# Ten decode units beside attention, two staging and result buffers, and another order of silu and output blocks

## The chip, the cores and the metric

The kernel runs on one core of one Trainium2 chip. The metric is the device time of a launch in microseconds, as the median of several runs.

## The reference

Attention over q, k, v (4 batches, 8 heads, 576 positions, 64 wide) has two parts that are added: a coarse attention on positions averaged in fours, repeated four times along the sequence, and a local one with a band of width 3 to either side. Its output, 2304 tokens of 512, goes through two dense layers:

```python
a = x @ w1                      # 512 -> 1024
b = x @ w2                      # 512 -> 1024
x = ((a * b) @ w3) @ w_out      # 1024 -> 1024 -> 512
h = x @ w_in                    # 512 -> 2048
out = (h * (1.0 / (1.0 + np.exp(-h)))) @ w_out2   # 2048 -> 512
```

The weights arrive as 64-bit floating point numbers.

## The kernel before

**Numbers.** The weights are decoded on the chip from 64-bit to 32-bit values with integer operations (absolute value on ScalarE, clamp, shift and two merges on VectorE). Where a product is to be exact enough, each operand is split in a high and a low part (hi, lo), and TensorE makes three products (hi·hi, lo·hi, hi·lo; `PASSES`).

**Opening (to about 111 us).** w3 @ w_out is made into one matrix (`wprime`, L449), while the first of the 16 attention units run.

**Middle (111 to 504 us).** A unit u of attention is two heads of one batch. Its work is cut in 48 steps: `scores(u)` (D1, L1), `turn(u)` (D2, L2: transposes; `pool_v`: two adds on GpSimd that make `vd`, L236 and L239) and `sums(u - 1)` (D3, L3). D3 (L304) multiplies the transposed coarse weights `EdT` (two ScalarE copies, L298) with `vd` into one of two PSUM buffers and copies the result out on VectorE (L316); L3 (L369) makes the local part, and `make_x` adds both. In between lie 192 slots: an ab slot is 12 matmuls of one half of x against w1 or w2 (L540), a y slot 12 matmuls of (a·b) with the joined matrix (L580), for 320 or 256 tokens. y goes to DRAM (`ydram`).

**Background decode.** The second layer pair's weights are 16 units (`units`: 8 of w_in, 8 of w_out), each loaded to a staging tile (`bg_load`, `sw`, 1 MB in two DMAs), decoded and split (`bg_steps`), and stored to DRAM (`wsd`, `wod`) from a result tile (`res`). A unit of w_in has two results, one of 768 and, after sums of its blocks (`mix`), one of 1024 columns. The staging tile and the result tile have one buffer each in the pool `stg`; the decoded values alternate between two. `starts` says at which slot each unit begins: 14 + 18n for six units, 122 + 6n for ten. The steps stand 1 to 11 slots behind that, the load of the next unit behind the last merge.

**What sets the order.** Outside the last stage the framework places instructions by priority and by the time at which it expects their inputs; each engine then runs its own list strictly in order. `behind` puts the steps of a slot no earlier than the last marked instruction of the slot ahead; it does not bound them from the other side. All DMAs are issued by SyncE, in order.

**Turn to the last stage.** At slot `bg_end` (185) `open_y` closes the pool `stg` and opens `yp` in its place; y of the first tile of 768 tokens is loaded there (`y_load`), combined on GpSimd (`y_mix`, L752) and split (`y_high`, ScalarE, L757; `y_rest`, VectorE or GpSimd, L763).

**Last stage (from L956, order written out by hand on TensorE, VectorE, ScalarE, GpSimd).** Three tiles of 768 tokens times eight units of 256 hidden columns. A unit (`h_unit`) makes its 2x2 block product with seven chains of 6 matmuls (L916, a Strassen-like scheme) on two PSUM buffers, and VectorE sums them (L905) to the halves `cf` (ready after chain 4) and `cg` (after chain 6). `silu` takes the sigmoid on ScalarE (L886); `rest`, one chain later, multiplies (L891), rounds (L892), and subtracts the low part on GpSimd (L893). Behind each chain follow `run_out` blocks: a block is three matmuls (L852) of the unit before's half and a quarter of w_out, first the first half's six, then the second's. At a tile's end, in the first unit of the next one, the six accumulators are evicted (L859, L861) and stored.

Of the kernel before, what the change touches and what calls it, by code (L numbers as in the profile page):

```python
# [8 lines left out]
F32 = mybir.dt.float32  # L9
F32R = mybir.dt.float32r  # L10
# [19 lines left out]
I32 = mybir.dt.int32  # L30
# [5 lines left out]
def tile_model(ctx: ExitStack, tc: tile.TileContext, qk, vw, vr, w12, w3t, wo, wb, out):  # L36
# [3 lines left out]
    def pool(stack, name, side, space=None, bufs=1):  # L40
        kw = {} if space is None else {"space": space}
        return stack.enter_context(
            tc.tile_pool(name=name, bufs=bufs, side=side, reuse_waits="tile", **kw)
        )
# [3 lines left out]
    wpool = pool(ctx, "wpool", "left", bufs=4)  # L48
    s_stg, s_att, s_x, s_w3, s_c = (ExitStack() for _ in range(5))
    stg = pool(s_stg, "stg", "left", bufs=2)  # L50
    s_stg2, s_cb = ExitStack(), ExitStack()
    att = pool(s_att, "att", "left", bufs=2)
    stg2 = pool(s_stg2, "stg2", "left", bufs=2)
    xpool = pool(s_x, "xpool", "right", bufs=12)
    w3pool = pool(s_w3, "w3pool", "right", bufs=2)

# [59 lines left out]
    n_loads = [0]  # L116

    def stage(home, name):
        return home.tile([P, 2, 512, 2], I32, tag="st", name=name, bufs=1)

    def load_w(key):
        n = n_loads[0]
        home = homes[n % len(homes)]
        n_loads[0] += 1
        if not wide:
            st = home.tile([P, 2, 512], F32, tag="st", name="st", bufs=1)
        elif n < 4 or 6 <= n < 10:
            st = wpool.tile([P, 2, 512, 2], I32, tag="wB" if n < 4 else "wC", name="lent")
        else:
            st = stage(home, "st")  # L130
        for t in range(2):
            src = w_source(key, t)
            if wide:
                nc.sync.dma_start(st[:, t].rearrange("p n w -> p (n w)"), src.bitcast(I32))
            else:
                nc.sync.dma_start(st[:, t], src)
        raw[key] = st
# [270 lines left out]
    def turn(u):  # L408
        D2(u)
        L2(u)  # L410
        pool_v(u)
        load_vr(u + 1)
        pool_qk(u + 1)

    def sums(u):
        D3(u)
        L3(u)
        load_vw(u + 1)

# [76 lines left out]
        else:  # L496
            load_to(n + 2)

    homes.append(stg2)
    load_qk(0)  # L500
    load_to(1)
    load_vr(0)
# [115 lines left out]
    def bg_load(n):  # L618
        if n >= len(units):
            return  # L620
        kind, p = units[n]
        if wide:
            st = stg.tile([P, 2, 512, 2], I32, tag="st", name="sw", bufs=1)
        else:
            st = stg.tile([P, 2, 512], F32, tag="st", name="sw", bufs=1)
        for t in range(2):
            src = wb[2 * p + kind, :, t * 512:(t + 1) * 512]
            if wide:
                nc.sync.dma_start(st[:, t].rearrange("p n w -> p (n w)"), src.bitcast(I32))
            else:  # L630
                nc.sync.dma_start(st[:, t], src)
        bg["st", n] = st

    def bg_steps(n):

        kind, p = units[n]
        hold = {}

        def first():
            st = bg.pop(("st", n))  # L640
            v = stg.tile([P, 1024], I32, tag=("dec", "dec2")[n % 2], name="dec", bufs=1)
            hold["v"], hold["f"] = v, v.bitcast(F32)
            if wide:
                st = st.rearrange("p t n w -> p (t n) w")
                hold["st"] = st
                nc.scalar.activation(hold["f"], st[:, :, 1].bitcast(F32), AF.Abs)
            else:
                nc.scalar.copy(hold["f"], st.rearrange("p t n -> p (t n)"))

        def clamp():  # L650
            if wide:
                nc.vector.tensor_scalar(
                    out=hold["f"], in0=hold["f"], scalar1=E_LOW, scalar2=E_HIGH,
                    op0=ALU.max, op1=ALU.min,
                )
                nc.vector.tensor_scalar(
                    out=hold["v"], in0=hold["v"], scalar1=3, scalar2=0x3FFFFFF8,
                    op0=ALU.logical_shift_left, op1=ALU.bitwise_and,
                )

        def top():
            if wide:
                nc.vector.scalar_tensor_tensor(
                    out=hold["v"], in0=hold["st"][:, :, 1], scalar=-0x40000000, in1=hold["v"],
                    op0=ALU.bitwise_and, op1=ALU.bitwise_or,
                )

        def low():
            if wide:
                nc.vector.scalar_tensor_tensor(  # L670
                    out=hold["v"], in0=hold["st"][:, :, 0], scalar=29, in1=hold["v"],
                    op0=ALU.logical_shift_right, op1=ALU.bitwise_or,
                )
            bg_load(n + 1)

        def high(w):
            hold["r"] = stg.tile([P, 2, 1024], F32R, tag="res", name="res", bufs=1)[:, :, :w]
            nc.scalar.copy(hold["r"][:, 0], hold["f"][:, :w])  # L678

        def rest(w):  # L680
            r = hold["r"]
            nc.vector.tensor_tensor(  # L682
                out=r[:, 1], in0=hold["f"][:, :w], in1=r[:, 0].bitcast(F32), op=ALU.subtract
            )

        def store(where):
            nc.sync.dma_start(
                where.rearrange("p (l n) -> p l n", l=2), hold["r"].bitcast(F32)
            )

        def mix():
            f = hold["f"]
            a11, a12, a22, a21 = (f[:, 256 * i:256 * i + 256] for i in range(4))
            for out_, in0, in1, op in (
                (a22, a21, a22, ALU.add), (a21, a11, a21, ALU.subtract),
                (a11, a22, a11, ALU.subtract), (a12, a12, a11, ALU.subtract),
            ):
                nc.vector.tensor_tensor(out=out_, in0=in0, in1=in1, op=op)

        steps = [(0, first), (1, clamp), (2, top), (3, low)]  # L700
        if kind:
            steps += [(5, lambda: high(1024)), (6, lambda: rest(1024)),
                      (7, lambda: store(wod[p]))]
        else:
            steps += [(5, lambda: high(768)), (6, lambda: rest(768)),
                      (7, lambda: store(wsd[p, :, 0:1536])), (7, mix),
                      (9, lambda: high(1024)), (10, lambda: rest(1024)),
                      (11, lambda: store(wsd[p, :, 1536:3584]))]
        return steps

    plan = {}
# [1 line left out]
    def at(slot, fn):  # L713
        plan.setdefault(slot, []).append(fn)

    starts = [14 + 18 * n for n in range(6)] + [122 + 6 * n for n in range(10)]
    at(13, lambda: bg_load(0))
    for n in range(len(units)):
        for k, fn in bg_steps(n):
            at(starts[n] + k, fn)  # L720
# [68 lines left out]
    end_a = max(i for i, g in enumerate(kinds) if g is not None)  # L789

    def open_y():
        s_stg.close()
        yp.append(pool(ctx, "yp", "left"))
        y_load(0)
# [20 lines left out]
    for i, slot in enumerate(slots):  # L815
        run_plan(36 + i)
        if i == 13:
            assert n_jobs[0] == len(jobs)
            s_stg2.close()
            homes[:] = [stg]  # L820
            cpool_b[0] = pool(s_cb, "cpool_b", "right", bufs=2)
        behind(plan.pop(i, []))
        slot()
        n = 36 + max(0, i - 3) if i < 40 else 72 + ((i - 39) * 36) // 46
        run_steps(n // 3 + 1)
        if not opened and done_steps[0] == NSTEP:
            s_att.close()
            opened = True
            assert i < bg_end, (i, bg_end)
    for i in sorted(plan):  # L830
        behind(plan.pop(i))
    assert opened
# [51 lines left out]
    def silu(u, half, c):  # L884
        sg = temp("sg", f"{u}_{half}", 2, 2 * NH)
        nc.scalar.activation(sg, c, AF.Sigmoid)  # L886
        g = b2.tile([P, 2, 2 * NH], F32R, tag="g", name=f"g{u}_{half}", bufs=5)
        G[u, half] = g

        def rest():  # L890
            nc.vector.tensor_tensor(out=sg, in0=c, in1=sg, op=ALU.mult)  # L891
            nc.vector.tensor_copy(g[:, 0], sg)  # L892
            nc.gpsimd.tensor_tensor(  # L893
                out=g[:, 1], in0=sg, in1=g[:, 0].bitcast(F32), op=ALU.subtract
            )

        after(1, rest)

    def h_unit(u):
        t, p = divmod(u, 8)  # L900
# [8 lines left out]
        for i, (name, w, c) in enumerate(CH):  # L909
# [38 lines left out]
                after(3, lambda i=i: y_rest(t + 1, i))  # L948
            if 2 <= p < 6 and i == 5 and t + 1 < NT:
                y_mix(t + 1, p - 2)  # L950
            run_out((2, 2, 2, 2, 2, 1, 1)[i])
        wc_load(u + 2)
        if p == 1 and t + 1 < NT:
            y_load(t + 1)
# [2 lines left out]
    with tc.manual_schedule(engines={E.PE, E.DVE, E.Activation, E.Pool}):  # L957
        for u in range(NUN):
            h_unit(u)
            assert not todo  # L960
            todo.extend((u, half, j) for half in range(2) for j in range(6))
        for _ in range(3):
            next_chain()
        assert not later
        todo.sort(key=lambda x: (x[2], x[1]))
        run_out(12)


# [54 lines left out]
```

## Time and profile before

| | |
|---|---|
| Median of 3 runs | 967.16 us (966.91 to 969.13) |
| Profiled execution | 970.69 us |
| its span | 968.9 us |
| its mean granted TensorE clock | 0.962 |
| TensorE busy | 874.4 us, 90% of the span |
| VectorE, ScalarE, GpSimd busy | 536.6, 300.2, 282.4 us |

The span is what the trace covers, from the first instruction to the last; 1.8 us lie around it. Times in the trace count from the span's start. "Busy" of TensorE is not its best rate, since matmuls overlap; its rate is read from starts of equal groups. L12 is line 12 of the kernel before.

### The profile page before, as it was taken

How to read it: one execution, taken by the hardware profiler on the slowest of the kernel's cores; microseconds unless marked ns; L12 is line 12 of the kernel's file. 1: busy time of each engine (PE TensorE's matmuls, PEld its weight loads, DVE VectorE, ACT ScalarE, POOL GpSimd, SP SyncE). 2: the span in 40 equal slices, each digit the busy share in tenths (PEclk: the TensorE clock that was granted, in tenths of full speed). 3: DMA queues.
4: the chain of work that ended last, by engine and by line, in shares of the span. 5: the costliest groups of instructions: out<-in, count | busy, mean ns of one | idle time of the engine just before them, and what ended most of it. 6: DMA issues, size and time to landing. Idle time of an engine off the chain costs nothing.

```text
span 968.9 us, 17419 instructions
## 1 busy us (share of the span) xinstructions
PE 874.4 (90%) x7104; PEld 761.9 (79%) x7104; DVE 536.6 (55%) x850; ACT 300.2 (31%) x865; POOL 282.4 (29%) x226
## 2 busy tenths in 40 slices
PE   3999999999999999999970699999899999999996
PEld 2555689889998999999870578888788888888884
DVE  5999987545546462766552444545536456543432
ACT  5665654543344444333221211113111022111101
POOL 2000244333424242311210622434314335121311
PEclk9999989999999999999995599999999999999998
DMA  9926544343341521368789332424624232632403
GB/s 341 336 92 206 180 146 135 120 148 114 131 168 56 196 97 64 130 228 307 262 296 366 126 128 76 153 76 145 210 80 151 77 128 101 164 130 76 153 0 66
DMA packets 39729, 149.17 MB, mean 154 GB/s; under 512 B 4448, under 2 KB 11616, under 8 KB 33504
## 3 DMA queue, kind: packets, MB, share of 16 engines
q1 hardware_dynamic: 39648, 148.05, 45.1%
q8 instruction: 56, 0.92, 0.4%
q14 instruction: 25, 0.20, 0.1%
HBM read 115.52 MB, written 32.51 MB: 153 GB/s over the span
## 4 chain that ended last, share of the span: by engine, by line
PE 60%; DVE 15%; DMA 9%; POOL 6%; issue 4%; ACT 4%; SPq 0%; POOLq 0%; ACTq 0%; DVEq 0%
PE o L852 17%; PE h L916 13%; PE ab L540 13%; PE y L580 7%; POOL g L893 4%; DMA sw<-wb 4%; PE wp L449 4%; PE ol L369 2%; DVE sg L891 2%; DMA wsd<-res 1%; DVE g L892 1%; DVE u L905 1%; PE tl L345 1%; DVE cg L905 1%; ACT band L250 1%
## 5 line engine op out<-in xcount | busy, mean ns | idle before, releaser
L852 PE MATMUL o<-wo,g 128*128 128x512 f32 x864 | 238.1, 403 | 24.3 <-POOL g L893 23.0
L852 PEld LDWEIGHTS o<-wo,g 128*128 128x128 f32 x864 | 160.7, 190 | 59.3 <-POOL g L893 32.3
L893 POOL TENSOR_TENSOR g<-sg,g 128x768 fp32r<-128x768 f32 x48 | 88.1, 1835 | 277.9 <-DVE g L892 277.9
L916 PE MATMUL h<-yc,wcb 128*128 128x384 f32 x576 | 120.1, 345 | 8.3 <-POOL yc L763 6.6
L916 PEld LDWEIGHTS h<-yc,wcb 128*128 128x128 f32 x576 | 106.6, 193 | 17.4 <-POOL yc L763 7.1
L916 PE MATMUL h<-yc,wca 128*128 128x384 f32 x432 | 90.7, 346 | 30.7 <-ACT yc L757 28.7
L565 POOL TENSOR_TENSOR c<-cf,c 128x320 fp32r<-128x320 f32 (+1 forms) x64 | 66.5, 1039 | 172.0 <-DVE c L564 145.1
L540 PE MATMUL ab<-x,w_wB 128*128 128x320 f32 (+1 forms) x768 | 112.5, 301 | 0.8 <-ACT x L393 0.4
L540 PE MATMUL ab<-x,w_wA 128*128 128x320 f32 (+1 forms) x768 | 111.7, 302 | 1.4 <-DVE cf L554 0.6
L580 PE MATMUL y<-c,w_wC 128*128 128x320 f32 (+1 forms) x768 | 109.0, 298 | 2.3 <-POOL c L565 1.3
L916 PEld LDWEIGHTS h<-yc,wca 128*128 128x128 f32 x432 | 79.8, 193 | 38.3 <-ACT yc L757 28.9
L540 PEld LDWEIGHTS ab<-x,w_wA 128*128 128x128 f32 x768 | 105.5, 192 | 3.3 <-DVE cf L554 0.8
L540 PEld LDWEIGHTS ab<-x,w_wB 128*128 128x128 f32 x768 | 105.4, 191 | 1.7 <-ACT x L393 0.7
L580 PEld LDWEIGHTS y<-c,w_wC 128*128 128x128 f32 x768 | 103.1, 188 | 3.2 <-POOL c L565 1.6
L886 ACT ACTIVATE sg<-cf 128x768 f32<-128x768 f32 x24 | 20.3, 847 | 224.5 <-DVE cf L905 224.5
L905 DVE TENSOR_TENSOR u<-h,u 128x384 f32<-128x384 f32 x48 | 26.7, 557 | 80.9 <-PE h L916 80.9
L449 PE MATMUL wp<-w_wo,w_w 128*128 128x512 f32 x128 | 62.1, 628 | 2.4 <-DVE w_w L177 2.0
L554 DVE TENSOR_TENSOR cf<-ab,af 128x320 f32<-128x320 f32 (+1 forms) x64 | 28.9, 451 | 55.4 <-PE ab L540 52.2
L886 ACT ACTIVATE sg<-cg 128x768 f32<-128x768 f32 x24 | 20.3, 846 | 87.6 <-DVE cg L905 87.6
L250 ACT ACTIVATE band<-band,sm 128x38 f32<-128x38 f32 x144 | 44.9, 317 | 5.7 <-DVE sm L246 5.2
L682 DVE TENSOR_TENSOR res<-dec,res 128x1024 fp32r<-128x1024 f32 (+1 forms) x24 | 28.1, 1170 | 33.2 <-ACT res L678 33.0
L891 DVE TENSOR_TENSOR sg<-cg,sg 128x768 f32<-128x768 f32 x24 | 35.0, 1458 | 20.4 <-ACT sg L886 20.4
(115 smaller groups left out, 1067.2 us busy)
## 6 DMA issues: line engine op xcount, KB each, us to landing
wcb<-wsd SPq DMA_DIRECT2D x24, 1024.0 KB, 6.2
wca<-wsd SPq DMA_DIRECT2D x24, 768.0 KB
sw<-wb SPq DMA_DIRECT2D x32, 512.0 KB, 4.9
qk<-qk SPq DMA_DIRECT2D x16, 579.0 KB, 4.8
wsd<-res SPq DMA_DIRECT2D x8, 1024.0 KB, 6.1
wod<-res SPq DMA_DIRECT2D x8, 1024.0 KB, 5.7
wo<-wod SPq DMA_DIRECT2D x8, 1024.0 KB, 5.1
st<-w SPq DMA_DIRECT2D x14, 512.0 KB, 5.0
```

Of the source, the lines that this page charges most:

```text
L250: nc.scalar.activation(E[:, j, :], src[:, j, :], AF.Exp, bias=nb[:, j:j + 1], scale=scale, accum_out=sv[:, j:j + 1],)
L449: nc.tensor.matmul(acc, lhsT=w3v[:, k, j * P:(j + 1) * P], rhs=wov[:, k, :], start=(gp == 0 and k == 0), stop=(gp == 3 and k == 1),)
L540: nc.tensor.matmul(acc[:, :N], lhsT=wv[:, i, w, kk, :], rhs=x[:, j, :], start=(n == 0), stop=(n == 11),)
L554: nc.vector.tensor_tensor(out=cf, in0=acc[:, :N], in1=C.pop("af"), op=ALU.mult)
L565: mark(nc.gpsimd.tensor_tensor(out=c[:, 1], in0=cf, in1=c[:, 0].bitcast(F32), op=ALU.subtract))
L580: nc.tensor.matmul(acc[:, :N], lhsT=WP[kf // 2][:, i, kf % 2, ec * P:(ec + 1) * P], rhs=c[:, j, :], start=(kf == 0 and n == 0), stop=(kf = ...
L852: nc.tensor.matmul(acc, lhsT=g[:, a, j * P:(j + 1) * P], rhs=w[:, b, half, :], start=(p == 0 and half == 0 and n == 0), stop=(p == 7 and h ...
L886: nc.scalar.activation(sg, c, AF.Sigmoid)
L891: nc.vector.tensor_tensor(out=sg, in0=c, in1=sg, op=ALU.mult)
L893: nc.gpsimd.tensor_tensor(out=g[:, 1], in0=sg, in1=g[:, 0].bitcast(F32), op=ALU.subtract)
L905: nc.vector.tensor_tensor(out=out_, in0=in0, in1=in1, op=op)
L916: nc.tensor.matmul(acc, lhsT=wc[w][:, a, c, kt * P:(kt + 1) * P], rhs=y[:, b, kt, :], start=(n == 0), stop=(n == 5),)
```

## The change

Two staging buffers serve the whole middle part (the extra pool `stg2`, closed at slot 13, is gone); units are loaded two ahead, one slot behind the last merge. Ten units start at 14 + 11n and six at 130 + 6n, so `bg_end` becomes 169. Once attention is done, a second result buffer in its memory (`late`) alternates with the first. The steps from `high` on come one slot earlier. D3 moves from `sums` to `turn`, ahead of `pool_qk`. In the last stage the first half's `rest` follows its sigmoid at once, the second half's one chain later as before; the last unit's low part is made on VectorE; there is no block behind chain 0 and there are two behind each other chain; the last twelve blocks run in the order first half, second half, no longer by column block.

```diff
     def stage(home, name):
-        return home.tile([P, 2, 512, 2], I32, tag="st", name=name, bufs=1)
+        return home.tile([P, 2, 512, 2], I32, tag="st", name=name, bufs=2)
...
         load_vr(u + 1)
+        D3(u)
         pool_qk(u + 1)
 
     def sums(u):
-        D3(u)
         L3(u)
...
         if wide:
-            st = stg.tile([P, 2, 512, 2], I32, tag="st", name="sw", bufs=1)
+            st = stage(stg, "sw")
...
-            bg_load(n + 1)
 
         def high(w):
-            hold["r"] = stg.tile([P, 2, 1024], F32R, tag="res", name="res", bufs=1)[:, :, :w]
+            home = stg
+            if late:
+                n_res[0] += 1
+                home = (stg, late[0])[n_res[0] % 2]
+            hold["r"] = home.tile([P, 2, 1024], F32R, tag="res", name="res", bufs=1)[:, :, :w]
...
-        steps = [(0, first), (1, clamp), (2, top), (3, low)]
+        steps = [(0, first), (1, clamp), (2, top), (3, low), (4, lambda: bg_load(n + 2))]
         if kind:
-            steps += [(5, lambda: high(1024)), (6, lambda: rest(1024)),
-                      (7, lambda: store(wod[p]))]
+            steps += [(4, lambda: high(1024)), (5, lambda: rest(1024)),
+                      (6, lambda: store(wod[p]))]
...
-    starts = [14 + 18 * n for n in range(6)] + [122 + 6 * n for n in range(10)]
+    N_EARLY = 10
+    starts = [14 + 11 * n for n in range(N_EARLY)]
+    starts += [130 + 6 * n for n in range(len(units) - N_EARLY)]
+    late, n_res = [], [0]
     at(13, lambda: bg_load(0))
+    at(13, lambda: bg_load(1))
...
             s_att.close()
+            late.append(pool(s_late, "late", "left"))
...
-            nc.gpsimd.tensor_tensor(
+            e = nc.vector if u == NUN - 1 else nc.gpsimd
+            e.tensor_tensor(
                 out=g[:, 1], in0=sg, in1=g[:, 0].bitcast(F32), op=ALU.subtract
             )
 
-        after(1, rest)
+        if half == 0:
+            rest()
+        else:
+            after(1, rest)
...
-            run_out((2, 2, 2, 2, 2, 1, 1)[i])
+            run_out(2 if i else 0)
...
-        todo.sort(key=lambda x: (x[2], x[1]))
         run_out(12)
```

## Rows read from the trace of the kernel before

**Rows 1.** Stages: length, busy us (x instructions) by engine, clock, DMA, GB/s

```profile
111.00:504.00 393.00, 383.47 (x4246) 365.68 (x4242) 227.48 (x405) 155.98 (x517) 130.39 (x131) 0.98 0.47 158
388.00:485.00 97.00, 94.78 (x768) 93.04 (x767) 62.17 (x99) 30.48 (x54) 22.37 (x22) 0.98 0.66 232
...
504.00:557.00 53.00, 14.88 (x49) 12.72 (x49) 19.27 (x23) 11.54 (x15) 16.59 (x9) 0.58 0.69 255
...
948.00:968.90 20.90, 12.46 (x39) 8.55 (x37) 5.06 (x8) 2.60 (x4) 3.61 (x2) 0.77 0.35 76
```

**Rows 2.** Order of time around 504 us: start, length, engine, line [idle before <-releaser]

```profile
495.15 8.78 PE L580 MATMUL y<-c,w_wC 128*128 128x256 f32 x72 [1.06 <-ACT af L547]
...
521.80 0.32 SPq L687 DMA_DIRECT2D wod<-res  x1
...
522.65 2.08 SPq L736 DMA_DIRECT2D yr<-ydram  x2
...
532.68 1.01 PE L916 MATMUL h<-yc,wca 128*128 128x384 f32 x2 [28.74 <-ACT yc L757]
...
545.59 3.57 POOL L763 TENSOR_TENSOR yc<-t,yc 128x768 fp32r<-128x768 f32 x2
...
554.02 2.59 PE L916 MATMUL h<-yc,wca 128*128 128x384 f32 x12
```

**Rows 3.** Groups by line: busy us, mean ns | idle before, by releaser

```profile
L852 PE MATMUL o<-wo,g 128*128 128x512 f32 x864 | 238.1, 403 | 24.3 <-POOL g L893 23.0 <-DVE g L892 0.9 <-PE h L916 0.2
...
L678 ACT CAST res<-dec 128x1024 fp32r<-128x1024 f32 (+1 forms) x24 | 23.5, 979 | 44.0 <-DMA wsd<-res 22.0 <-DMA wod<-res 15.4 <-DVE dec L670 6.7
...
L646 ACT ACTIVATE dec<-sw 128x1024 f32<-128x1024 f32 x16 | 18.2, 1140 | 29.6 <-DMA sw<-wb 27.4 <-DVE w_wA L190 2.2
...
L236 POOL TENSOR_TENSOR vr<-vr 72x512 f32<-72x512 f32 x12 | 17.6, 1463 | 94.4 <-DMA vr<-vr 94.3
...
L311 PE MATMUL od<-EdT,vd 72*64 72x144 f32 x128 | 12.3, 300 | 0.0
```

**Rows 4.** Order of time on SyncE: two of the loads of staged weights

```profile
473.76 1.32 SPq L629 DMA_DIRECT2D sw<-wb  x2
...
501.11 1.35 SPq L629 DMA_DIRECT2D sw<-wb  x2
```

**Rows 5.** Order of time within a unit of the last stage

```profile
564.84 1.22 PE L916 MATMUL h<-yc,wcb 128*128 128x384 f32 x6
...
565.90 1.56 PE L852 MATMUL o<-wo,g 128*128 128x512 f32 x6
...
567.29 1.22 PE L916 MATMUL h<-yc,wcb 128*128 128x384 f32 x6
...
569.20 0.85 ACT L886 ACTIVATE sg<-cf 128x768 f32<-128x768 f32 x1 [10.79 <-DVE cf L905]
...
571.95 0.95 DVE L891 TENSOR_TENSOR sg<-cf,sg 128x768 f32<-128x768 f32 x1
...
573.64 1.83 POOL L893 TENSOR_TENSOR g<-sg,g 128x768 fp32r<-128x768 f32 x1 [11.63 <-DVE g L892]
...
574.93 1.36 DVE L891 TENSOR_TENSOR sg<-cg,sg 128x768 f32<-128x768 f32 x1 [0.97 <-ACT sg L886]
...
575.53 1.43 PE L852 MATMUL o<-wo,g 128*128 128x512 f32 x5 [0.82 <-POOL g L893]
```

**Rows 6.** Order of time on GpSimd: first halves of two successive units

```profile
881.21 1.84 POOL L893 TENSOR_TENSOR g<-sg,g 128x768 fp32r<-128x768 f32 x1 [11.62 <-DVE g L892]
...
898.11 1.84 POOL L893 TENSOR_TENSOR g<-sg,g 128x768 fp32r<-128x768 f32 x1 [11.64 <-DVE g L892]
```

**Rows 7.** Order of time at the end, TensorE's output blocks

```profile
947.71 1.49 PE L852 MATMUL o<-wo,g 128*128 128x512 f32 x4
...
954.05 10.15 PE L852 MATMUL o<-wo,g 128*128 128x512 f32 x32 [1.47 <-POOL g L893]
```

**Rows 8.** Order of time in the second tile's first unit, an h chain

```profile
692.46 1.34 PE L916 MATMUL h<-yc,wca 128*128 128x384 f32 x6 [0.99 <-DVE cg L905]
```

More of the change, by code (lines that the diff above doesn't have):

```diff
@@ L50, in tile_model @@
     stg = pool(s_stg, "stg", "left", bufs=2)
-    s_stg2, s_cb = ExitStack(), ExitStack()
+    s_cb, s_late = ExitStack(), ExitStack()
     att = pool(s_att, "att", "left", bufs=2)
-    stg2 = pool(s_stg2, "stg2", "left", bufs=2)
     xpool = pool(s_x, "xpool", "right", bufs=12)
@@ L125, in load_w @@
         if not wide:
-            st = home.tile([P, 2, 512], F32, tag="st", name="st", bufs=1)
+            st = home.tile([P, 2, 512], F32, tag="st", name="st", bufs=2)
         elif n < 4 or 6 <= n < 10:
@@ L497, in ahead @@
             load_to(n + 2)
-    homes.append(stg2)
     load_qk(0)
@@ L622, in bg_load @@
         if wide:
-            st = stg.tile([P, 2, 512, 2], I32, tag="st", name="sw", bufs=1)
+            st = stage(stg, "sw")
         else:
-            st = stg.tile([P, 2, 512], F32, tag="st", name="sw", bufs=1)
+            st = stg.tile([P, 2, 512], F32, tag="st", name="sw", bufs=2)
         for t in range(2):
@@ L698, in mix @@
                 nc.vector.tensor_tensor(out=out_, in0=in0, in1=in1, op=op)
-        steps = [(0, first), (1, clamp), (2, top), (3, low)]
+        steps = [(0, first), (1, clamp), (2, top), (3, low), (4, lambda: bg_load(n + 2))]
         if kind:
-            steps += [(5, lambda: high(1024)), (6, lambda: rest(1024)),
-                      (7, lambda: store(wod[p]))]
-        else:
[L705 to L708, printed above, removed]
+            steps += [(4, lambda: high(1024)), (5, lambda: rest(1024)),
+                      (6, lambda: store(wod[p]))]
+        else:
+            steps += [(4, lambda: high(768)), (5, lambda: rest(768)),
+                      (6, lambda: store(wsd[p, :, 0:1536])), (6, mix),
+                      (8, lambda: high(1024)), (9, lambda: rest(1024)),
+                      (10, lambda: store(wsd[p, :, 1536:3584]))]
         return steps
@@ L791, in open_y @@
     def open_y():
+        s_late.close()
         s_stg.close()
@@ L818, in tile_model @@
             assert n_jobs[0] == len(jobs)
-            s_stg2.close()
-            homes[:] = [stg]
             cpool_b[0] = pool(s_cb, "cpool_b", "right", bufs=2)
@@ L827, in tile_model @@
             s_att.close()
+            late.append(pool(s_late, "late", "left"))
             opened = True
-            assert i < bg_end, (i, bg_end)
+            assert i < starts[N_EARLY], (i, starts[N_EARLY])
     for i in sorted(plan):
```

## The prediction

> **What bounds the kernel now.** I read the busy times by stage first [rows 1]. From 111 to 504 us TensorE is busy for 383.5 of 393 us, and in the last part of it, 388 to 485 us, for 94.8 of 97: the stage in which attention, ab and y share TensorE is bound by its matmuls. Then 504 to 557 us holds only 49 matmuls at a granted clock of 0.58, where 1.0 is the 2.4 GHz level and 0.5 the 1.2 GHz level: a hole. The last 21 us run at 0.77.
>
> The order of time shows what the hole waits for [rows 2]. The last y matmul ends at 495.15 + 8.78 = 503.9. The last background store (wod) goes out at 521.80, and the load of y, whose buffers lie in the memory of the closed staging pool, at 522.65. TensorE's first h matmul follows at 532.68, after 28.7 us of waiting for ScalarE's half of that y. GpSimd then prepares the other y parts until 545.59 + 3.57 = 549.2. The first product of the second unit ends at 554.02 + 2.59 = 556.6. So background decode is the last thing to end, and all else queues behind it.
>
> Why it is late: ScalarE waited 27.4 us for staged weights (L646) and 22.0 + 15.4 us for the one result buffer to be stored (L678) [rows 3], and loads of the next units go out at 473.76 and 501.11, two units apart, so 13.7 us a unit [rows 4] where the plan allows six slots. A slot is 12 matmuls, 1.5 to 1.8 us (the 72 of 495.15 took 8.78, that is 122 ns each at 256 columns [rows 2]; 320 columns scale to 152).
>
> Last I read one late unit [rows 5]. A chain of 6 h matmuls with two o blocks behind it repeats every 567.29 - 564.84 = 2.45 us, of which the chain alone is 565.90 - 564.84 = 1.06 and the 6 o matmuls 1.39 (232 ns each). In each unit the second o matmul waits for GpSimd's low part of the first half, which starts at 573.64 and takes 1.83: 0.82 us of idle TensorE at 575.53. A unit lasts 898.11 - 881.21 = 16.90 us [rows 6].
>
> **The change, part by part.** (1) *Ten units early, six late, two staging and two result buffers.* Nothing is computed that was not. Four units more lie beside attention, where VectorE is busy 227 of 393 us [rows 1]. With single buffers a unit in the late stage took 13.7 us, and VectorE was busy 62.2 of 97 us there; scaling all of that, the ab work too, to one unit per 9.5 us gives 62.2 x 13.7 / 9.5 = 90 of 97, an upper bound that still fits. So I charge nothing for VectorE; the cover is that TensorE has four accumulators in turn. If it is gone, the price is single waits like those of the stage now, which together are 393 - 383.5 = 9.5 us; I take 0 and keep -3 to +8.
>
> A rule speaks against this part. The row first: the same 128x768 product took 0.95 us alone and 1.36 beside GpSimd's subtraction [rows 5]. The Trainium skill, GPSIMD Engine Reference, section Key points, says that GpSimd shares its SBUF interfaces with VectorE and names contention with VectorE instructions that have two SBUF inputs; the row agrees, and decode has such instructions. If every one of them met GpSimd, the bound of 90 would grow by 1.36 / 0.95 to 129 of 97, the 57 us of the six late units by a third, and the sum would come to about 912; by the row alone, with GpSimd busy 22 of 97 us there [rows 1], it stays.
>
> (2) *The hole.* Slots 160 to 191 end with the last y matmul at 503.9. Counted back at 1.83 us for 320 columns and 1.48 for 256, slot 169, where y is now loaded, begins near 467, and slot 130, the first late unit, near 404. Six units of six slots end near 461, plus a lag I put at 5 to 10 us. The load took 532.68 - 522.65 = 10 us and the preparation 549.2 - 532.7 = 16.5 (GpSimd bound) [rows 2], so y is ready at 467 + 10 + 10 + 16.5 = 503: just in time, with no slack. I put 4 us of lateness (ends 0 and 16). The first unit then costs 7 x 1.06 = 7.4, and one new wait: its first-half silu now stands on VectorE ahead of the sums of chain 5, whose accumulator the second unit's first chain needs. Chain 4 ends at 5.3; sum 0.75, sigmoid 0.95, product 0.95, cast 0.56 and the two sums 1.1 end at 9.7, against 7.4: 2.3 us, once, since later units have o blocks there. With the 1.06 of the next chain that is 503.9 + 4 + 9.7 + 1.1 = 518.7 in place of 556.6: **-38** (-26 to -42).
>
> (3) *Prompt silu and no o blocks behind a unit's first product.* In the new order the first half's product can follow the sigmoid (569.20 + 0.85), about 570.1 instead of 571.95, so GpSimd's part starts about 1.8 us earlier, and the o blocks come one chain (1.06) later: 2.9 us against a wait of 0.82. The wait goes. Late next would be the sums of chain 5, pushed back about 1.6 us behind the product and cast; their accumulator is needed two chains on, 1.06 + 2 x 1.39 = 3.8 us later. A unit becomes 6 x 2.45 + 1.06 = 15.8: 1.1 x 23 = **-25** (-19 if only the visible 0.82 goes; -26). All 24.3 us that L852 waited [rows 3] are of this kind and of the tail.
>
> (4) *The end.* After the last chain's block, at 947.71 + 3 x 0.23 = 948.4, the old order needs the second half at its second block, waits for GpSimd, and runs 32 matmuls from 954.05 in 10.15 us, 317 ns each, at the lower clock [rows 7, 1]. The new order has 18 matmuls of the first half, 4.2 us, while VectorE makes the second half (sum, sigmoid, three passes of 0.56 to 0.95: about 3.9). 36 x 0.232 = 8.4 in place of 964.2 - 948.4 = 15.8; the six evictions then come 0.7 us apart with twelve stores behind them, for which I give back 0.5: **-7**.
>
> (5) *D3 a step earlier.* It issues four pairs of matmuls and a copy as before, and no DMA. Today it never waited (L311, 0.0 idle [rows 3]), as its inputs are a step old. Now TensorE could wait there for GpSimd's two adds behind it (L236 1.46 and a smaller one, at most 2.9 together [rows 3]), with ab matmuls queued behind. Twelve turns lie after the opening (L236 x12): 0 to 35 us, and below nothing by no more than a part of the 9.5 us of waits. I take 0, since outside the last stage instructions are placed where their inputs are expected ready. Where p = 0 a unit also evicts outputs; the first such place cost more than a normal unit (TensorE waited 0.99 at 692.46 [rows 8]); blocks now come closer there, I take -2 (+3 to -4).
>
> **Sum.** 38 + 25 + 7 + 2 = 72 off the span of 968.9 gives 897; with 970.69 - 968.9 = 1.8 around it 899. The median shown is 967.16, 0.36% below that execution: 899 x 0.9964 = 895.5, **895**.
>
> **Rivals.** *The hole closes only in part.* With late units still at 13.7 us, because stores and loads and not the buffers pace them, six end at 404 + 82 = 486, y is ready at 486 + 10 + 16.5 = 513 and TensorE idles 9 to 14 us and restarts at the lower level: 902 to 910, say 905. For it: no slack in part 2. Against it: both waits of ScalarE were on single buffers. *D3 holds TensorE* at most turns: 12 x 2.9 = 35, 930. Against it: L236's inputs are loaded a unit ahead. *The units keep their wait*, because VectorE now stands idle for the sigmoid ahead of the sums and the accumulators come late: 895 + 25 = 920. *Slower than before:* the same place, D3 on TensorE's queue, but each wait long enough that the clock falls to 1.2 GHz behind it, as it did behind the waits of the tail [rows 7]. It decides from 72 / 12 = 6 us a turn: 2.9 of wait and over 6 us of matmuls at half speed. With 7 us a turn the time is 979. The stage now holds a clock of 0.98 with 9.5 us of waits, which speaks against it.
>
> **How the numbers follow.** Forecast (886 to 902) 0.62, hole in part (905) 0.22, D3 (930) 0.07, units (920) 0.06, slower (979) 0.03. The range 885 to 914 takes in the first and nearly all of the second. A measurement of this kernel tells 0.3%, about 3 us, from no change. Every case but the last is faster by far: faster 0.96, same 0.01, slower 0.03.
>
> **What would show it.** Right: the h stage begins within some 5 us of the last y matmul at the 2.4 GHz level; wod's last store goes out before 475; POOL g no longer ends a wait of L852; the unit's period is 15.8; no clock drop in the tail; L311 idle near zero. Wrong: ScalarE's yc still releases the first h matmul after more than 10 us; L311 or L580 with tens of us of idle between 111 and 400; the last y matmul well past 504.

## The result, and the profile after

The changed kernel takes **898.1 us** (median of four, 895.1 to 901.3) where the kernel before took 968.1 in runs beside it: 0.927 of the time (95% interval 0.922 to 0.932). The forecast was 895, its range 885 to 914. The profiled execution is the fastest of the four, 895.1 us, with a span of 893.3 and a mean clock of 0.987; its counterpart of before had 970.7, 968.9 and 0.962. So 75.6 us of span have to be found.

I first read the stages of after, in the same columns as [rows 1]: from and to, length, busy us (x instructions) of TensorE, its weight loads, VectorE, ScalarE and GpSimd, then granted clock, DMA share and GB/s.

```profile
111.00:504.00 393.00, 382.10 (x4288) 363.72 (x4287) 252.60 (x420) 165.39 (x533) 158.97 (x139) 0.98 0.53 186
388.00:485.00 97.00, 94.78 (x776) 93.67 (x775) 65.59 (x93) 32.83 (x57) 38.28 (x29) 0.98 0.57 209
504.00:557.00 53.00, 51.06 (x250) 46.21 (x249) 23.64 (x40) 7.37 (x10) 12.88 (x7) 0.97 0.42 147
877.00:893.30 16.30, 8.85 (x38) 6.76 (x37) 4.55 (x6) 2.34 (x4) 0.00 (x0) 0.91 0.45 97
```

The stage up to 504 is as full as it was, with 25 us more work on VectorE. The hole from 504 to 557 is gone: 250 matmuls at a clock of 0.97 in place of 49 at 0.58. The end no longer runs at 0.77.

The order of time around 504 says what is late now (start, length, engine, line, operation, count, and in brackets the idle time before it and what ended it; SPq is SyncE's queue).

```profile
457.52 0.32 SPq L688 DMA_DIRECT2D wod<-res  x1
...
460.86 0.97 SPq L741 DMA_DIRECT2D yr<-ydram  x2
...
480.63 6.05 PE L538 MATMUL ab<-x,w_wA 128*128 128x256 f32 x36 [1.84 <-ACT yo L587]
...
483.67 1.84 POOL L768 TENSOR_TENSOR yc<-t,yc 128x768 fp32r<-128x768 f32 x1
...
486.51 11.52 PE L578 MATMUL y<-c,w_wC 128*128 128x256 f32 x96
497.87 2.25 PE L925 MATMUL h<-yc,wca 128*128 128x384 f32 x12
...
502.42 0.71 ACT L587 COPY yo<-y 128x256 f32<-128x256 f32 x2 [6.82 <-DMA ydram<-yo]
503.03 0.48 ACT L932 COPY p<-h 128x384 f32<-128x384 f32 x1
503.57 6.03 PE L925 MATMUL h<-yc,wcb 128*128 128x384 f32 x24 [3.44 <-ACT p L932]
509.44 1.21 PE L925 MATMUL h<-yc,wca 128*128 128x384 f32 x6
512.58 2.35 PE L925 MATMUL h<-yc,wca 128*128 128x384 f32 x12 [1.94 <-DVE cg L914]
```

The last background store leaves 64 us earlier than in [rows 2], and GpSimd's last part of y is made by 483.67 + 1.84 = 485.5, 12 us before the first h matmul needs it. That matmul follows the last y matmul (486.51 + 11.52 = 498.0) at once. The largest lateness left is new: ScalarE stands 6.82 us on a yo copy whose buffer is still being stored, the p copy waits behind it in ScalarE's order, and TensorE waits 3.44 us for p. The 24 matmuls after it take 6.03 us, at a lower clock (0.72 from 504 to 510 us).

Last, the groups by line, read as [rows 3], and the unit's period, read as [rows 6].

```profile
L857 PE MATMUL o<-wo,g 128*128 128x512 f32 x864 | 223.8, 395 | 0.0
...
L310 PE MATMUL od<-EdT,vd 72*64 72x144 f32 x128 | 11.4, 299 | 0.0
...
L235 POOL TENSOR_TENSOR vr<-vr 72x512 f32<-72x512 f32 x12 | 20.4, 1701 | 102.7 <-PE od L310 84.3 <-DMA vr<-vr 18.3
...
L644 ACT ACTIVATE dec<-sw 128x1024 f32<-128x1024 f32 x16 | 18.3, 1146 | 2.3 <-DVE w_wA L189 2.3
...
L679 ACT CAST res<-dec 128x1024 fp32r<-128x1024 f32 (+1 forms) x24 | 23.5, 980 | 39.3 <-DVE dec L668 16.3 <-DVE dec L699 12.9 <-DMA wsd<-res 5.9
```

```profile
811.31 1.85 POOL L899 TENSOR_TENSOR g<-sg,g 128x768 fp32r<-128x768 f32 x1 [9.02 <-DVE g L897]
...
827.09 1.85 POOL L899 TENSOR_TENSOR g<-sg,g 128x768 fp32r<-128x768 f32 x1 [9.04 <-DVE g L897]
```

The o matmuls (L852 of before) no longer wait at all, and a unit lasts 827.09 - 811.31 = 15.78 us instead of 16.90. ScalarE's wait for staged weights is gone, and of its waits for the result buffer 5.9 us are left; it waits for VectorE instead. D3's matmuls (L310) still wait for nothing; GpSimd now waits for them, 84 us in all, and between 111 and 400 us TensorE waits for GpSimd for 2.1 us (rows under "D3's place").

**Where the 75.6 us came from.** The first chain of the second unit ends at 556.6 before [rows 2] and at 512.58 + 2.35 - 1.09 = 513.8 after: 42.8. From there to the end of the o block behind the last chain it was 948.4 - 556.6 = 391.8 and is 877.3 - 513.8 = 363.5 (875.88 in the tail below, and six matmuls of 0.23): 28.3. The rest of the span was 20.5 and is 16.0: 4.5.

### The profile page after: what moved, and what is told of

It is laid out like the page before. It is cut to its first block, busy times and chain, and to the rows that moved or that the text cites. A ratio compares the mean times of both kernels' runs of the same rounds, so it can differ in the third digit from the quotient of the medians.

```text
span 893.3 us, 17448 instructions
## 1 busy us (share of the span) xinstructions
PE 852.6 (95%) x7104; PEld 749.6 (84%) x7104; DVE 532.6 (60%) x852; ACT 300.9 (34%) x865; POOL 286.2 (32%) x224
## 4 chain that ended last, share of the span: by engine, by line
PE 81%; DVE 8%; DMA 4%; ACT 2%; issue 2%; POOL 2%; SPq 1%; POOLq 0%; ACTq 0%; DVEq 0%
PE o L857 21%; PE ab L538 20%; PE h L925 19%; PE y L578 9%; PE wp L448 4%; PE ol L368 2%; PE tl L344 1%; PE sd L276 1%; PE s L325 1%; DMA out<-os 1%; PE od L310 1%; PE td L293 1%; DMA ydram<-yo 1%; DMA st<-w 1%; DMA yr<-ydram 1%
## 5 line engine op out<-in xcount | busy, mean ns | idle before, releaser
L857 PE MATMUL o<-wo,g 128*128 128x512 f32 x864 | 223.8, 395 | 0.0
L857 PEld LDWEIGHTS o<-wo,g 128*128 128x128 f32 x864 | 160.3, 188 | 27.2
L899 POOL TENSOR_TENSOR g<-sg,g 128x768 fp32r<-128x768 f32 x46 | 85.0, 1847 | 260.2 <-DVE g L897 244.6
L538 PE MATMUL ab<-x,w_wB 128*128 128x320 f32 (+1 forms) x768 | 114.3, 303 | 3.6 <-POOL x L393 2.1
L563 POOL TENSOR_TENSOR c<-cf,c 128x320 fp32r<-128x320 f32 (+1 forms) x64 | 73.2, 1145 | 117.9 <-DVE c L562 109.3
L925 PE MATMUL h<-yc,wca 128*128 128x384 f32 x432 | 83.6, 337 | 1.9 <-DVE cg L914 1.9
L925 PEld LDWEIGHTS h<-yc,wca 128*128 128x128 f32 x432 | 76.8, 188 | 6.2 <-DVE cg L914 2.3
L235 POOL TENSOR_TENSOR vr<-vr 72x512 f32<-72x512 f32 x12 | 20.4, 1701 | 102.7 <-PE od L310 84.3
L448 PEld LDWEIGHTS wp<-w_wo,w_w 128*128 128x128 f32 x128 | 23.8, 197 | 27.9 <-issue 23.9
```

Source lines behind the costliest of these rows:

```text
L235: side().tensor_tensor(out=r[:, :, 0:2, :], in0=r[:, :, 0:2, :], in1=r[:, :, 2:4, :], op=ALU.add)
L448: nc.tensor.matmul(acc, lhsT=w3v[:, k, j * P:(j + 1) * P], rhs=wov[:, k, :], start=(gp == 0 and k == 0), stop=(gp == 3 and k == 1),)
L538: nc.tensor.matmul(acc[:, :N], lhsT=wv[:, i, w, kk, :], rhs=x[:, j, :], start=(n == 0), stop=(n == 11),)
L563: mark(nc.gpsimd.tensor_tensor(out=c[:, 1], in0=cf, in1=c[:, 0].bitcast(F32), op=ALU.subtract))
L857: nc.tensor.matmul(acc, lhsT=g[:, a, j * P:(j + 1) * P], rhs=w[:, b, half, :], start=(p == 0 and half == 0 and n == 0), stop=(p == 7 and h ...
L899: e.tensor_tensor(out=g[:, 1], in0=sg, in1=g[:, 0].bitcast(F32), op=ALU.subtract)
```

## Experiments

The kernel before was run beside every group: 967.2 (e1 to e4), 968.7 (e5 to e8) and 969.5 (e9 to e12). Ratios are to that, with 95% intervals.

**The two halves alone.** e1 has only the edits of the last stage, e2 only those of the middle part.

```diff
 e1: before, with only
+            e = nc.vector if u == NUN - 1 else nc.gpsimd
...
+        if half == 0:
+            rest()
...
+            run_out(2 if i else 0)
...
-        todo.sort(key=lambda x: (x[2], x[1]))
 e2: after, with these lines back as before
```

> The kernel before with the last stage of the changed one alone (prompt silu of the first half, no blocks behind chain 0, the last unit's low part on VectorE, last twelve blocks by half). Theory: the hole at 504 us stays as it is, each of 23 units loses its 1.1 us wait and the tail 4 to 7 us, so 30 to 33 us off the kernel before: 935 to 938 us, period of a unit 15.8. Rival (the two parts of the change help each other, so that the units keep a wait when they start cold behind the hole): 945 or more.

> The changed kernel with the last stage of the kernel before. Theory: the hole is closed (TensorE idle at most 6 us between the last y and the first h matmul and the chains behind it), but every unit waits for GpSimd again and lasts 16.9 us: 927 to 932 us. Its gain and that of the last stage alone should add up to that of the whole change within some 4 us. Rival: the gains overlap, and this run is below 922 or above 936.

Measured: e1 938.4, ratio 0.970 (0.968 to 0.973); e2 929.3, ratio 0.961 (0.958 to 0.963). The o matmuls of e1, then those of e2, by line:

```profile
L852 PE MATMUL o<-wo,g 128*128 128x512 f32 x864 | 223.8, 395 | 0.0
```

```profile
L857 PE MATMUL o<-wo,g 128*128 128x512 f32 x864 | 239.0, 404 | 24.7 <-POOL g L898 23.5 <-DVE g L897 0.9 <-PE h L921 0.2
```

Both are about as expected (935 to 938 and 927 to 932). The wait for GpSimd belongs to the last stage's edits and to nothing else: e1 loses it while its hole stays (first h matmul at 533.75 after 28.48 us for ScalarE's yc), e2 keeps it while its hole is closed. The gains, 28.8 and 37.9, add to 67 of the 70 us of the whole, so the two halves hardly touch each other.

**D3's place.** The last y matmul ended at 498.0, not at 503.9, which the forecast had not seen. e3 puts D3 back into `sums`; e11 moves it alone, in the kernel before.

```diff
 e3: after, with
-        D3(u)
         pool_qk(u + 1)
...
     def sums(u):
+        D3(u)
 e11: before, with the reverse
```

> The changed kernel with D3 back in the step of the sums, one step later. Theory: D3 was free in either place (TensorE never waited at L310), so the same time within 3 us, and the last y matmul at 498 as in the changed kernel. Rival: the earlier D3 is what brought the end of the middle stage from 504 to 498, then 901 to 905 and the last y matmul near 504.

> The kernel before with D3 moved to the earlier step and nothing else. Theory: the middle stage ends some 4 to 5 us earlier (last y matmul near 499), but the hole ends with the background stores, so it only grows by as much: the time of the kernel before within 4 us (963 to 971). Rival: attention that ends earlier lets the background units end earlier too, and 4 us or more show in the time.

Measured: e3 903.4, ratio 0.933 (0.931 to 0.936): the rival of its text came true, not its theory. Its last y matmul ends at 491.05 + 11.52 = 502.6. What TensorE waited for between 111 and 400 us, in e3 and then in after (us in total, times, longest):

```profile
PE ol L368 <- DVE ods L315: 3.4, 4, 1.4
PE tl L344 <- issue: 0.7, 3, 0.3
PE ab L538 <- DVE w_wA L189: 0.2, 1, 0.2
```

```profile
PE ab L538 <- POOL x L393: 2.1, 2, 1.6
PE td L293 <- DVE xf L382: 1.1, 1, 1.1
PE ab L538 <- ACT x L392: 1.1, 1, 1.1
PE tl L344 <- issue: 0.7, 3, 0.3
```

With D3 in its old place the ol matmuls (L3) wait four times for VectorE's ods, the copy at the end of D3; that row is not in after. But waits don't make the difference: the rows add to 4.3 us in e3 and to 5.0 in after. What differs is TensorE's own time for the ol matmuls (busy us, mean ns), e3 first:

```profile
L368 PE MATMUL ol<-ET,vw 38*64 38x32 f32 x1152 | 35.8, 226 | 3.5 <-DVE ods L315 3.4
```

```profile
L368 PE MATMUL ol<-ET,vw 38*64 38x32 f32 x1152 | 24.7, 222 | 0.0
```

A single ol matmul lasts about the same in both (226 and 222 ns), but in after they overlap more, and the 1152 of them keep TensorE busy for 11.1 us less. Every run with D3 at its new place has 23.8 to 24.8 us here, every run with D3 at its old place (before, e1, e3) 33.5 to 35.8. D3's result takes one of the two PSUM buffers that the ol matmuls use, and the wait for ods is the wait for that buffer; that this is also why they overlap less was not tested. Not all of the 11.1 us reaches the end of the stage: the y matmuls end 4.6 us later in e3, and its median is 5.3 above that of after (the two intervals just meet). So D3's move is worth about 5 us here. In the kernel before it can't be told from nothing: e11 took 967.5, ratio 0.999 (0.997 to 1.001). Its trace:

```profile
488.30 8.78 PE L580 MATMUL y<-c,w_wC 128*128 128x256 f32 x72 [1.02 <-ACT af L547]
...
515.12 0.32 SPq L687 DMA_DIRECT2D wod<-res  x1
...
526.15 1.01 PE L916 MATMUL h<-yc,wca 128*128 128x384 f32 x2 [29.07 <-ACT yc L757]
```

The y matmuls end 6.8 us earlier than in [rows 2], and TensorE then waits 29.07 us where it waited 28.74: earlier y matmuls alone gain nothing while background decode ends last. In this one execution the last store left 6.7 us earlier too and the span was 5.1 us shorter, which the medians, 1.9 apart, don't bear out. Whether D3's place moves background decode stays open.

**What closes the hole: buffers or early units?** Between before and after, three things changed at once for background decode: ten early units instead of six, a second staging buffer with loads two ahead, and a second result buffer. e9 takes the staging alone; e6 both buffers at the old slots; e5 ten early units with one result buffer; e10 ten early units and both buffers, but loads one ahead. The last stage, D3 and the decode steps, which come one slot earlier, are those of after in all four.

```diff
 e6: after, with
-    N_EARLY = 10
-    starts = [14 + 11 * n for n in range(N_EARLY)]
-    starts += [130 + 6 * n for n in range(len(units) - N_EARLY)]
+    starts = [14 + 18 * n for n in range(6)] + [122 + 6 * n for n in range(10)]
 e5: after, with
-            if late:
+            if late and False:
 e9: both of these
 e10: after, with
-        steps = [(0, first), (1, clamp), (2, top), (3, low), (4, lambda: bg_load(n + 2))]
+        steps = [(0, first), (1, clamp), (2, top), (3, low), (3, lambda: bg_load(n + 1))]
...
-    at(13, lambda: bg_load(1))
```

> Six early and ten late units as in the kernel before, one result buffer, but two staging buffers loaded two ahead (the run with six early units, its second result buffer taken away). Theory after the earlier runs: with two staging buffers the early units and the second result buffer stand in for each other, and with neither the 15 late results come 8 us apart as in the run with one result buffer, so the last store goes out near 505, the h chains start in earnest 24 us behind it, and the time is 918 to 928. Rival: two staging buffers alone close the hole, last store below 485, 900 or less.

> The changed kernel with the slots of the kernel before: six units early (14 + 18n), ten late (122 + 6n), so that y is loaded at slot 185, but with two staging and two result buffers. Theory: the late units keep up at about 10 us each, the last store is near 490, and the hole is what loading and preparing y takes behind slot 185, 15 to 20 us: 912 to 920. Rival (the number of early units is what matters, since the late ones are limited by stores and loads, not by buffers): last store near 515, hole near 40 us, 930 or more.

> The changed kernel without the second result buffer: ten units early, two staging buffers, one result buffer throughout. Theory: the six late units again wait for each store, about 9 results 7 to 9 us apart (65 to 80 us from 404), so the last store goes out at 470 to 485 instead of 457.5, and y is ready at 497 to 512: 898 to 908 us. Rival: with two staging buffers the one result buffer is enough, the last store stays below 465 and the time at 898.

> The changed kernel with each unit loaded one ahead, behind the last merge of the unit before, as in the kernel before; ten early units and the second result buffer kept. Theory: with ten early units six late ones at up to 13.7 us end near 404 + 80 = 484 at the latest, as late as in the run with six early units, so the time is 898 to 905. Rival: loading two ahead is what closes the hole, last store past 490, 910 or more.

Measured, with the time of the last background store and ScalarE's waits for result buffers between 380 and 510 us (behind stores to wsd, and after the plus sign to wod):

```
kernel  early  results  time   ratio (95%)            last store  result waits
e9      6      1        920.1  0.951 (0.947 to 0.954)  500.96     27.3 + 9.7
e6      6      2        897.9  0.926 (0.924 to 0.929)  480.78      2.1
e5      10     1        898.8  0.928 (0.923 to 0.932)  472.09     15.7 + 3.0
e10     10     2        895.7  0.926 (0.921 to 0.931)  457.13      0
after   10     2        898.1  0.927 (0.922 to 0.932)  457.52      3.7
```

In e9 the staging wait is gone and the wait has moved to the one result buffer. Its time is 18 us less than that of e1 (938.4), which has the same last stage; the earlier decode steps and D3's move, which gained nothing in e11, are in that difference too. The hole stays:

```profile
480.14 11.53 PE L578 MATMUL y<-c,w_wC 128*128 128x256 f32 x96
511.41 1.01 PE L923 MATMUL h<-yc,wca 128*128 128x384 f32 x2 [19.74 <-ACT yc L760]
...
526.17 4.11 PE L923 MATMUL h<-yc,wcb 128*128 128x384 f32 x13 [6.61 <-POOL yc L766]
```

A second result buffer takes 22 us off that (e6), and no more comes of the four further early units: after is equal to e6 although its last store leaves 23 us earlier. With ten early units the second result buffer is worth nothing (e5), nor are loads two ahead (e10). Beside the second staging buffer either of the two changes is enough, and the slack beyond that buys nothing. Ten early units and two results with one staging buffer were not run; e10, whose loads go out one ahead, comes nearest. Its time lies 2 us below what was expected of it, and its last store left at 457, where 484 at the latest was expected. How e5 and e6 stay level with after, though y is prepared later in both, is seen in the order of time, of e5 first and then of e6:

```profile
484.83 6.08 PE L578 MATMUL y<-c,w_wC 128*128 128x256 f32 x50
500.15 7.21 PE L578 MATMUL y<-c,w_wC 128*128 128x256 f32 x37 [9.24 <-POOL c L563]
507.19 2.24 PE L925 MATMUL h<-yc,wca 128*128 128x384 f32 x12
509.28 4.35 PE L925 MATMUL h<-yc,wcb 128*128 128x384 f32 x24
```

```profile
481.38 11.52 PE L578 MATMUL y<-c,w_wC 128*128 128x256 f32 x96
492.75 0.52 PE L923 MATMUL h<-yc,wca 128*128 128x384 f32 x2
494.36 2.03 PE L923 MATMUL h<-yc,wca 128*128 128x384 f32 x10 [1.09 <-POOL yc L766]
504.76 6.67 PE L923 MATMUL h<-yc,wcb 128*128 128x384 f32 x24 [8.37 <-ACT p L930]
```

e5 pays 9.24 us in the middle of the y matmuls (GpSimd has y's preparation ahead of the sum c) and then runs h without a wait. e6 pays 8.37 later, for p, but had begun its last y matmuls 5 us earlier; after lost 1.84 us to a wait at 480.63, with a clock of 0.83 from 480 to 490 us, which e6 does not show. All three start the 24 matmuls within 503.6 to 509.3 us. That is a balance of different waits, which I had not forecast: the expectations of e6 were missed on both sides.

**The two edits of a unit.** e7 keeps the prompt silu and the old block counts; e8 keeps the new block counts and takes both halves one chain later.

```diff
 e7: after, with
-            run_out(2 if i else 0)
+            run_out((2, 2, 2, 2, 2, 1, 1)[i])
 e8: after, with
-        if half == 0:
-            rest()
-        else:
-            after(1, rest)
+        after(1, rest)
```

> The changed kernel with the old number of blocks behind each chain (2, 2, 2, 2, 2, 1, 1), the prompt silu kept. Theory: the prompt silu alone is 1.8 us earlier against a wait of 0.8, so the units keep a period of 15.8 and the time is that of the changed kernel within 3 us. Rival: a wait of 0.2 us or more remains per unit (product and cast behind the sigmoid end too late for the second block), 903 or more.

> The changed kernel with the silu of both halves one chain later as before, no blocks behind chain 0 kept. Theory: the first blocks come 1.06 us later than before, against a wait of 0.8 to 1.1, so the wait is all but gone: period 15.8 to 15.9, and the first unit's 1.9 us wait at chain 0 of the second unit goes too: the changed kernel within 3 us. Rival: both halves of the edit are needed, 0.3 us or more remain per unit, 905 or more.

Measured: e7 899.7, ratio 0.928 (0.924 to 0.932), e8 893.2, ratio 0.922 (0.919 to 0.925). The o matmuls of e7, then of e8, wait for nothing, and the period is 15.79 and 15.78:

```profile
L857 PE MATMUL o<-wo,g 128*128 128x512 f32 x864 | 229.8, 398 | 0.0
```

```profile
L857 PE MATMUL o<-wo,g 128*128 128x512 f32 x864 | 224.0, 395 | 0.0
```

Each edit alone removes the whole wait of 1.1 us a unit; the second of them adds nothing. e8 lies 4.9 us below after, more than the 3 allowed for, yet the intervals overlap and the two profiled executions (895.8 and 895.1 us) don't show it; what is seen is its first unit waiting 0.60 us for cg instead of 1.94.

**What is left.** e4 gives yo four buffers instead of two, the last output blocks six instead of three, and takes the first half of unit 0 one chain later; e12 adds to it the casts of y two slots later, to remove the 1.84 us before 480.63.

```diff
 e4: after, with
-            yo = cpool.tile([P, TOK[0]], F32, tag="yo", name=f"yo{b}_{h}_{ec}")[:, :N]
+            yo = cpool.tile([P, TOK[0]], F32, tag="yo", name=f"yo{b}_{h}_{ec}", bufs=4)[:, :N]
...
-            o = b2.tile([P, 512], F32, tag="o", name=f"os{t}_{j}", bufs=3)
+            o = b2.tile([P, 512], F32, tag="o", name=f"os{t}_{j}", bufs=6)
...
-        if half == 0:
+        if half == 0 and u:
 e12: e4, with
-        at(bg_end + 1 + i // 2, lambda i=i: y_high(0, i))
-        at(bg_end + 2 + i // 2, lambda i=i: y_rest(0, i))
+        at(bg_end + 3 + i // 2, lambda i=i: y_high(0, i))
+        at(bg_end + 4 + i // 2, lambda i=i: y_rest(0, i))
```

> The changed kernel with four instead of two buffers for the copied-out y (yo), six instead of three for the copied-out outputs (o), and the first unit's first half again one chain later. Theory: ScalarE's wait of 6.8 us for y stores at 502 goes, and with it TensorE's 3.4 us and the slow clock behind it (5 us); the sums of chain 5 no longer stand behind the silu in the first unit (2 us); the last evictions no longer wait for stores (2.7 us). Together 7 to 10 us less than the changed kernel: 888 to 891. Rival: the stores are late because the DMA engines are full at 500 us, and what waits next (the first unit's weights, the loads of w_out) takes most of it back: 895 or more, with other waits in the first two units.

> The run with more buffers, with the ScalarE casts of y and the low parts behind them two slots later, so that they no longer stand on ScalarE waiting for GpSimd's combinations ahead of a copy of y. Theory: TensorE's 1.8 us wait for that copy at 480 and the slow clock behind it (1.6 us) go, the prepared y is still in time: 2 to 4 us less than the run with more buffers, 882 to 884. Rival: the copy waits elsewhere or the y comes too late, 885 or more.

Measured: e4 **885.7**, ratio 0.916 (0.914 to 0.918), which beats after as well and is 2 us better than expected; e12 886.3, ratio 0.914 (0.911 to 0.917), so what it adds gains nothing. The 1.8 us wait for yo is still there, and ScalarE still has the last cast (479.47 us) ahead of the copy of y (480.21): the edit did not change the order that it was meant to change, and the idea behind it stays untested. e4 in order of time:

```profile
498.85 4.35 PE L925 MATMUL h<-yc,wcb 128*128 128x384 f32 x24
...
506.24 1.32 PE L925 MATMUL h<-yc,wca 128*128 128x384 f32 x6 [0.61 <-DVE cg L914]
...
867.01 9.97 PE L857 MATMUL o<-wo,g 128*128 128x512 f32 x42
```

The 24 matmuls neither wait nor run slow: 3.44 + (6.03 - 4.35) = 5.1 us less, and 1.3 in the first unit. Two buffers of yo, not the preparation of y, were the cause of the lateness in after. The end tells the opposite of the second edit, the six o buffers. The evictions of e4 wait for TensorE alone, while in after they wait for stores; first after, then e4:

```profile
875.88 9.97 PE L857 MATMUL o<-wo,g 128*128 128x512 f32 x42
883.00 7.51 SPq L869 DMA_DIRECT2D out<-os  x12
886.02 0.69 DVE L864 COPY os<-o 128x512 f32<-128x512 f32 x1 [2.24 <-DMA out<-os]
887.35 0.58 ACT L866 COPY os<-o 128x512 f32<-128x512 f32 x1 [2.98 <-DMA out<-os]
...
```

```profile
874.12 7.52 SPq L869 DMA_DIRECT2D out<-os  x12
...
875.61 0.69 DVE L864 COPY os<-o 128x512 f32<-128x512 f32 x1 [0.71 <-PE o L857]
...
```

Yet from the start of the 42 matmuls to the end of the span it is 893.3 - 875.88 = 17.4 us in the one and 884.4 - 867.01 = 17.4 in the other. The twelve stores leave 0.63 us apart whatever the buffers are, and the span ends 2.8 us after the last has been issued in both. So the o buffers gave nothing, and the end is bound by the stores. In after SyncE is held 0.54 to 0.60 us by each issue from the second store on, which starts at 883.52 us, when the DMA engines have moved nothing yet (share 0.00 from 883 to 884 us); from 885 to 891 us they show 0.90 to 1.01. Whether SyncE's issuing or the DMA engines set the pace was not separated. Of the 8.9 us between the two spans the rows explain 5.1 + 1.3, and 1.1 more by last y matmuls that end at 496.9 instead of 498.0; the medians lie 12.4 apart.

## Why the prediction was right, and where its steps were not

**The hole: 42.8 us against 38 (bounds 26 and 42, so just past the upper one).** The mechanism was as told: background decode no longer ends last, and h starts on the last y matmul's heels. Two terms were off. The last y matmul, taken at 503.9, ended 5.9 us earlier; most of that is D3's move (e3 gives 4.6), which I had costed at 0 with a gain excluded but for part of 9.5 us of waits. That step looked at waits alone, and the gain lies in TensorE's busy time: the ol matmuls took 33.5 us before and take 24.7. The way from there to the end of the second unit's first chain was 15.8 us against 14.8: the first unit's new wait for VectorE's sums measured 1.94 for 2.3, and the lateness 5.1 for 4.

**The lateness had the wrong cause.** I had y ready at 503 with no slack; it was ready at 485.5. The last store was put at 466 to 471 and left at 457.5, and the load landed in some 7 us instead of 10. That the lateness still had about the right size was luck; it came from a place that the working did not look at: the yo copies with their two buffers, whose stores stood among the wo loads and the load of y. From 486 to 504 us the DMA engines show a share of 1.00 at 401 GB/s in after. Even my rival "hole in part", which rests on the same slack, fails by the 12 us that the slack really was.

**The cause of the old hole was told too narrowly.** "Single buffers" holds at six early units, where the second result buffer is worth 22 us (e9 and e6). But ten early units with one result buffer do the same (e5); I had credited the pair, and the working had no term that tells which part does it.

**The units: 28.3 against 27** (25 and 2 for the tile change). The period of 15.78 was forecast as 15.8, from the chain and block times of [rows 5]. The sum counted two edits for one wait, though: e7 and e8 show that either is enough. At the tile change the largest wait is 0.82 us for p, at 643 us, so the 2 was right in direction.

**The end: 4.5 against 7.** The matmuls came as forecast, 42 in 9.97 us or 237 ns each, at a clock of 0.91 over the window and without the old 317 ns. What was mis-sized is the give-back: 0.5 for "twelve stores behind them". From the last o matmul to the end it is 893.3 - 885.85 = 7.45 us where before it was 968.9 - 964.2 = 4.7: 2.7. Faster matmuls had taken the stores' cover away, and the six evictions that I let come 0.7 us apart met stores 0.63 us apart, two for each eviction.

**The rest held.** Staging and VectorE cost nothing that shows: TensorE's busy time of 388 to 485 us is 94.78 in both. The product took 0.96 us alone in the changed last stage and 2.61 beside GpSimd's yc at 624.65, but the period of the units stayed at 15.78 (in that very unit 636.03 - 620.25, read as [rows 6]), and 898 came, not the 912 that I had worked out for contention at every such instruction, without a chance of its own. (By its own terms that sum is 895 + 57 / 3 = 914; and the terms before the first unit's end add to 9.6, not 9.7.) The Trainium skill, GPSIMD Engine Reference, section Key points, names this contention of GpSimd with VectorE; the row agrees that it is there, and the period shows that nothing on the path waited for it.

```profile
624.65 2.61 DVE L896 TENSOR_TENSOR sg<-cg,sg 128x768 f32<-128x768 f32 x1
```

None of the other rivals occurred: L310 idles 0.0 (D3 does not hold TensorE), and L857 idles 0.0 (the units do not keep their wait).

**How the sum met the median.** The terms were 4.8 too small for the hole and 1.3 for the units, and 2.5 too large for the end: 3.6 of span, 893.3 in place of 897. The step to the median then erred the other way. I had taken it 0.36% below the profiled execution, as before; here it lies 0.34% above it (898.1 to 895.1). That the sum met the median within 3 us is in part these errors cancelling.

## What to carry to other kernels

When a long background job ends late, list what lets it end earlier (its starts, staging, results) and price each alone; here more staging and either of the other two would have done, and the slack of the third bought nothing. Before charging nothing for a step that is moved, look at the busy time of the groups beside it and not only at their waits: D3's move took 9 to 11 us of TensorE's time off the ol matmuls. Before shortening a wait, ask what stands in order behind the next engine's slowest store: the copies of yo, a buffer that no part of the change touched, cost 5 us, and two more buffers brought it back. And at a kernel's end, count the stores by the interval at which they leave before crediting faster matmuls.

## What the runs showed of the hardware

- Small stores wait long when the DMA engines are full: with a share of 1.00 at 401 GB/s, ScalarE's yo copy stood 6.82 us behind a 128 KB store of y. With four buffers the same stretch, 486 to 504 us, ran at 1.03 and 420 GB/s and TensorE did not wait.
- The twelve 128 KB output stores at the end keep their pace of 0.63 us, about 207 GB/s. That is half of the 401 GB/s above, and still they set the end.
- The same 128x768 product of VectorE took 0.96, 1.36 and 2.61 us: alone, beside GpSimd's subtraction [rows 5], and beside its yc.
- A wait of 3.44 us was followed by 24 matmuls at 0.25 us each in place of 0.18, the clock from 503 to 510 us being 0.76 on the mean, between the 1.2 GHz level (0.5) and the 2.4 GHz level (1.0). The 1.84 us wait at 480 us was followed by 36 matmuls in 6.05 us in after (clock 0.83 from 480 to 490 us), but in 4.52 us in e12 (clock 1.00), so an equal wait did not always bring the lower clock.
- The same 1152 small matmuls (ol, 38x32) kept TensorE busy for 24 to 25 us or for 34 to 36, at 220 to 226 ns each, with D3 away from them or right ahead of them.
